# Weight splits three to five slots ahead, background work bounded by the next evictions, and h's buffers moved by 192 bytes

## The chip, the cores and the metric

The kernel runs on one core of one Trainium2 chip. The metric is the device time in microseconds (us) of one execution. The engines are TensorE (PE, matmuls; PEld its weight loads), VectorE (DVE), ScalarE (ACT), GpSimd (POOL) and SyncE (SP, which only issues DMAs here). Each engine works through its own queue in program order and waits at semaphores for the others.

## The reference

For x of 2048 rows and 576 columns, the output is the sum of x, an attention branch and a dense branch, both on the layer-normalised x:

```
xn  = (x - mean(x)) / sqrt(var(x) + 1e-5)
q, k, v = split(xn @ wqkv)                    # 32 heads of 18 columns
o   = softmax(q . k[s - 2j]) v[s - 2j], j=0..7  # 8 keys, two rows apart, masked where s - 2j < 0
out = x + o @ wo + relu(xn @ w1) @ w2         # w1: 576 x 4608, w2: 4608 x 576
```

## The kernel before, in words

**Number format.** Each fp32 operand is written as a high part (rounded for TensorE's fp32r format) and a low part (the rest). A product is high x high + high x low + low x high. Making both parts of a tile is called a split: ScalarE copies the high part, VectorE subtracts it from the source for the low part (function `two`, lines 158 to 164; its VectorE instruction is line 163). Weight tiles are split this way before use: `w1t` (128 x 640, for one block of 128 hidden columns) and `w2t` (128 x 576). The activations h are split on their way out of PSUM: `hhi` by ScalarE with the relu (line 588), `hlo` by VectorE (line 591).

**Slots.** The rows are cut into two phases of 1024 (even and odd rows), each into four blocks of 256 (`tb`). The 4608 hidden columns are cut into 36 tiles of 128; three tiles (`f` = 0, 1, 2) form a chunk. One slot is one hidden tile times one block; a chunk is 12 slots (tb outer, f inner), a phase has 12 chunks, and there are 288 slots, numbered n = 0 to 287. In the body (line 849), slot n issues, in this order:

- the weight splits that are due (`run_splits(n)`);
- half of the h matmuls of a pair of later slots. An even n does the first half for slots n+2 and n+3 together (28 matmuls of 64 rows, two at a time on the two halves of the array), the following odd n the second half (26), and then `hhi` and `hlo` of both;
- in eight slots out of 24, a block of the qkv product (`qkv_tile`, 28 or 26 matmuls of 432 columns, tiles `pm<-wq,xT`);
- `o_two(n)`: 24 matmuls of h(n) with w2 into `po`; at f = 2 VectorE adds the finished `po` to x in four pieces (line 699, `x<-po,x`), which also frees `po` for the next block;
- background work of VectorE (`run_bg`): the attention of one unit of 8 heads, in 77 small steps (products `pr<-qo,k`, sums `lg<-pr`, the softmax on `lg`, products `pr<-lg,v`, tree adds `pr<-pr` and `qo<-pr`). One unit's qkv comes every 24 slots (first at slots 7 to 14 of a phase), and its attention is queued at the 9th slot after.

**What sets the order.** All of it is put out by one Python planner. It keeps two clocks, `t["pe"]` and `t["dve"]`, that grow by a fixed cost for each instruction, and `run_bg(margin)` puts out background steps as long as VectorE's clock would stay within `margin` of TensorE's. The margin is `M` (line 847): 3.0 us after f = 0 and f = 2, 1.5 us after f = 1, and 1.5 us around the product with wo. A split's slot comes from the list `plan` (lines 725 and 726). With s the first slot that uses hidden tile f of a chunk, w1's splits stand at s-5, s-4 and s-2 for f = 0, 1, 2, and w2's at s-3, s-1 and s. In slots counted from the chunk's first slot these are -5, -3, 0 for w1 and -3, 0, 2 for w2. The h matmuls that first use w1's tiles f = 0 and 1 are those of slot -2 of that count, and those that first use f = 2 are those of slot 0. `stage_more` issues a split's DMA into a buffer `st` three splits ahead.

**PSUM.** h has two banks under the name `ph`; a second pair of banks, `pm`, alternates with it except in and right after the slots with a qkv block, where `pm` holds qkv. There each pair of slots uses the same two `ph` banks, so that the next first half waits until `hhi` and `hlo` of the pair before are read out.

Of the kernel before, what the change touches and what calls it, by code (L numbers as in the profile page):

```python
# [10 lines left out]
F32 = mybir.dt.float32  # L11
# [7 lines left out]
P = 128  # L19
# [7 lines left out]
C = 3  # L27
# [5 lines left out]
WO_CHUNK = 10  # L33
# [8 lines left out]
HEADW = (-9, -8, -7, -6, -5, -4)  # L42
# [16 lines left out]
def tile_body(ctx: ExitStack, tc: tile.TileContext, x, wqkv, wo, w1, w2, out):  # L59
# [12 lines left out]
    SPC = NTB * C  # L72
    SPP = NCH * SPC

    ctx.enter_context(tc.manual_schedule())
    pool = lambda name, bufs, **k: ctx.enter_context(tc.tile_pool(name=name, bufs=bufs, **k))
# [7 lines left out]
    w2p = pool("w2p", C + 1)  # L84
    wqp = pool("wqp", 1)
    stp = pool("stp", 5)
    hp = pool("hp", LAG + 1)
    prp = pool("prp", 2)
    lgp = pool("lgp", 1)
# [23 lines left out]
    t = {"pe": 0.0, "dve": 0.0}  # L113
# [16 lines left out]
    def dve(n):  # L130
        t["dve"] += (n + 130) / 960.0
# [16 lines left out]
    def run_splits(n):  # L148
        nonlocal step_now
        while staged and staged[0][0] <= n:  # L150
            step_now, split, st = staged.popleft()
            split(st)
            stage_more()
# [362 lines left out]
    def run_bg(margin):  # L516
        while bg and t["dve"] + bg[0][0] / 960.0 <= t["pe"] + margin:
            n, f, a = bg.popleft()
            f(*a)
            dve(n)  # L520
# [44 lines left out]
    slots = [(ph, c, tb, f) for ph in range(NPH) for c in range(NCH) for tb in range(NTB) for f in range(C)]  # L565
# [34 lines left out]
    def h_mm(n):  # L600
        h_terms(n, TERMS)
        h_out(n)
# [3 lines left out]
    def h_two(g, second):  # L606


        def run(n, terms):
            ph, c, tb, f = slots[n]  # L610
            w, xt = W1[ph, c, f], XT[ph, tb]
            return [
                (HP[n], w[:, b // 5, (b % 5) * P : (b % 5 + 1) * P], xt[:, a, :], not second and j == 0, second and j == len(terms) - 1, TBN)
                for j, (a, b) in enumerate(terms)
            ]

        if not second:
            HB["m"] = not HB["m"] and not busy_m.intersection((g - 3, g - 2, g - 1))
            for n in (g, g + 1):
                HP[n] = ps_m.tile([P, TBN], F32, name="pm") if HB["m"] else ps_h.tile([P, TBN], F32, name="ph")  # L620
            HB["ins"] = mm_rows((run(g, LOWER_MORE), run(g + 1, UPPER_MORE)))
            return
        mm_rows((run(g + 1, LOWER), run(g, UPPER)), HB["ins"])
        h_out(g)
        h_out(g + 1)
# [6 lines left out]
    def o_two(n):  # L632


        ph, c, tb, f = slots[n]
        hi, lo = H.pop(n)
        w = W2[ph, c, f]
        with_wo = c == WO_CHUNK and f == 1
        if f == 0:
            o_tiles(n)  # L640

        def run(k, h, upper):
            cs, first = slice(k * P, (k + 1) * P), k == upper
            z = [(l[:, cs], w[:, b, CUT[h]]) for l, b in ((hi, 0), (hi, 1), (lo, 0))]
            if with_wo:
                more = wo_run(ph, 2 * tb + k, h, (UPPER_MORE if upper else LOWER_MORE) if first else (UPPER if upper else LOWER), upper)
                z = z + more
            return [
                (PO[k, h], l, r, f == 0 and first and j == 0, f == C - 1 and not first and j == len(z) - 1, CUT[h].stop - CUT[h].start)
                for j, (l, r) in enumerate(z)  # L650
            ]

        for j in range(4):
            k, h = divmod(j, 2)
            behind = PB[j - 2] if j > 1 else PB[3] if j == 0 and f else None
            PB[j] = mm_rows((run(k, h, False), run(1 - k, h, True)), behind)
        if with_wo:
            for k in range(2):
                OT.pop((ph, 2 * tb + k))
        o_out(n, rows=True)  # L660
# [25 lines left out]
    def o_out(n, which=range(2), rows=False):  # L686
        ph, c, tb, f = slots[n]
        if f < C - 1:
            return
        end = n == len(slots) - 1  # L690
        order = [(k, h) for k in which for h in range(2)]
        if rows:
            order.sort(key=lambda z: z[1])
        elif end:
            order.sort(key=lambda z: (z[0], -z[1]))
        for k, h in order:
            i = 2 * tb + k
            acc, cols = X[ph, i], CUT[h]
            nc.vector.tensor_tensor(acc[:, cols], PO[k, h], acc[:, cols], op=ALU.add)  # L699
            dve(cols.stop - cols.start)  # L700
            if end and k:
                (nc.scalar if h else nc.sync).dma_start(o_v[ph, i][:, cols], acc[:, cols])
            elif c == NCH - 1 and (k, h) in (order[-1], order[-2 if rows else 1]):
                nc.sync.dma_start(o_v[ph, i], acc)
# [4 lines left out]
    def at(n, f, *a):  # L709
        todo.setdefault(n, []).append((f, a))  # L710
# [3 lines left out]
    def late(n, f, *a):  # L714
        todo_late.setdefault(n, []).append((f, a))

    plan = []
    busy_m = set()
    for ph in range(NPH):
        b = ph * SPP  # L720
        for c in range(NCH):
            for f in range(C):
                s = b + c * SPC + f
                first = ph == c == 0
                plan.append((HEADW[f] if first else s + (-5, -4, -2)[f], w1_task, ((ph, c, f), c * C + f)))
                plan.append((HEADW[3 + f] if first else s + (-3, -1, 0)[f], w2_task, ((ph, c, f), c * C + f)))
        for u in range(NU):
            s = b + UNIT0 + u * UNIT_STEP
            plan.append((s - 5, wq_tasks, ((ph, u), u)))
            for i in range(NI):  # L730
                at(s + i, qkv_tile, ph, u, i)
                busy_m.add(s + i)
            late(s + NI + 1, attention, ph, u)
        plan.append((b + WO_CHUNK * SPC - 6, wo_tasks, (ph,)))
        for i in range(NI):
            z = b + WO_CHUNK * SPC + C * (i // 2) + 1
            out_at, in_at, parts_at = (z + k[i % 2] for k in WO_STEPS)
            late(out_at, wo_a, ph, i)
            late(in_at, wo_f, ph, i)
            at(parts_at, wo_s, ph, i)  # L740
        if ph + 1 < NPH:
            e = b + SPP - SPC
            for i in range(NI):
                if i >= len(XT_STEPS):
                    z = e + 3 + 2 * i - (i == NI - 1)
                    at(z - 6, load_x, ph + 1, i)
                    late(z - 2, stats, ph + 1, i)
                    late(z - 1, norm, ph + 1, i)
                    at(z + 1, make_xt, ph + 1, i)
                    busy_m.add(z + 1)  # L750
                    continue
                load, first, second, send, back, parts = (e + k for k in XT_STEPS[i])
                at(load, load_x, ph + 1, i)
                late(first, stats, ph + 1, i, False, True)
                late(second, norm_turned, ph + 1, i)
                late(send, xt_a, ph + 1, i)
                at(back, xt_f, ph + 1, i)
                at(parts, xt_s, ph + 1, i)
# [70 lines left out]
    h4[0]()  # L829
    h4[1]()  # L830
    o_out(2, (0,))
    x4 = make_xt(0, 4, parts=True)
    for f in x4[:3]:
# [10 lines left out]
        (late if k else at)(z, {"stats": stats, "norm": norm, "xt": make_xt}[op], 0, *a)  # L844
    for tb in range(NTB):
        late((4, 4, 6, 7)[tb], twin, tb)
    M = (3.0, 1.5, 3.0)
    AT_WO = range(WO_CHUNK * SPC - 4, (WO_CHUNK + 1) * SPC)
    for n in range(FIRST, len(slots)):
        run_splits(n)  # L850
        g = n - n % 2 + LAG
        if n < ROW0:
            h_mm(n + LAG)
        elif g < len(slots):
            h_two(g, n % 2 == 1)
        for f, a in todo.pop(n, []):
            f(*a)
        if ROW0 - 1 <= n < len(slots) - C:
            o_two(n)
        else:  # L860
            o_mm(n, n != HALVED)
        if n == HALVED:
            o_out(n, (0,))
        for f, a in todo_late.pop(n, []):
            f(*a)
        if n == HALVED:
            o_out(n, (1,))
        run_bg(1.5 if n % SPP in AT_WO else M[slots[n][3]])
    assert not todo and not todo_late and not bg and not tasks and not staged


# [24 lines left out]
```

## Time and profile before

| | before |
|---|---|
| median of 3 runs | 1310.32 us (1308.1 to 1313.4) |
| the profiled execution | 1312.54 us |
| its span, first to last instruction | 1310.7 us |
| mean granted TensorE clock (1 is 2.4 GHz) | 0.963 |
| busy: PE, PEld, DVE, ACT, POOL | 1203.6, 1182.5, 804.0, 287.1, 44.5 us |

The time of an execution is its span and a small rest around it (1.8 us here). A busy TensorE is not TensorE at its peak: matmuls overlap, and at half the clock the same work is busy for twice as long. The views of the trace that are used further down: the waits of one engine (who waited for whom, in total), the timeline (instructions in order of time, like ones merged; in brackets the idle time before the row and what ended it), and the page.

### The profile page before, as it was taken

The page shows a single profiled execution, that of the slowest core. Times are in us where ns is not written, and L with a number is a line of the kernel's source. Part 1 is how long each engine was busy: PE and PEld are TensorE (multiplying, and loading weights), DVE is VectorE, ACT ScalarE, POOL GpSimd, SP SyncE. Part 2 cuts the span into 40 slices and gives each one's busy share as a digit, 9 for nine tenths or more (in the row PEclk, how much of TensorE's full clock was granted, in tenths as well). Part 3 has the DMA queues.
Part 4 walks back from the last instruction along what each step waited for, and adds up shares of the span by engine and source line. Part 5 has one row for each costly group of instructions (what it writes and reads, how often), then busy time and mean ns, then how long its engine had stood idle before and what let it go on. Part 6 is the DMA issues. An engine that isn't in the chain of part 4 may idle for free.

```text
span 1310.7 us, 38255 instructions
## 1 busy us (share of the span) xinstructions
PE 1203.6 (92%) x17114; PEld 1182.5 (90%) x17114; DVE 804.0 (61%) x1457; ACT 287.1 (22%) x756; POOL 44.5 (3%) x60
## 2 busy tenths in 40 slices
PE   9998989979898998899989989899798989988998
PEld 8998989979898898899979989899798988988998
DVE  7346866775685766753662468576766857667523
ACT  5311212221212111211432121112112121112110
POOL 3100000000000000000010000000000000000000
PEclk9999989999998999999989999898999989999999
DMA  5221212212221211544651222122022212116411
GB/s 173 69 62 42 63 38 66 71 29 61 55 68 31 61 40 49 134 91 110 149 148 40 62 55 68 30 56 79 21 62 55 68 31 61 40 48 141 88 50 74
DMA packets 149939, 89.70 MB, mean 68 GB/s; under 512 B 58528, under 2 KB 133536, under 8 KB 149776
## 3 DMA queue, kind: packets, MB, share of 16 engines
q1 hardware_dynamic: 146816, 78.61, 22.4%
q10 hardware_dynamic: 2960, 8.65, 2.3%
q8 instruction: 134, 2.20, 0.7%
q14 instruction: 29, 0.24, 0.1%
HBM read 67.90 MB, written 11.14 MB: 60 GB/s over the span
## 4 chain that ended last, share of the span: by engine, by line
PE 75%; DVE 17%; issue 2%; DMA 2%; SPq 1%; ACT 1%; POOL 0%; DVEq 0%; POOLq 0%; ACTq 0%
PE po L126 33%; PE pm L126 23%; PE ph L126 18%; DVE x L699 5%; DVE w1t L163 2%; DVE w2t L163 2%; DVE pr L491 2%; DVE lg L464 2%; DVE pr L498 1%; DMA st<-in_w 1%; DVE hlo L591 1%; DVE pr L461 1%; PE po L116 0%; DVE lg L486 0%; SPq L353 0%
## 5 line engine op out<-in xcount | busy, mean ns | idle before, releaser
L126 PE MATMUL po<-w2t,hhi 64*128 64x256 f32 (+1 forms) x4448 | 467.0, 298 | 0.3 <-DVE w2t L163 0.3
L126 PEld LDWEIGHTS po<-w2t,hhi 64*128 64x128 f32 x4448 | 381.6, 190 | 2.4 <-issue 0.8
L126 PE MATMUL ph<-xT,w1t 64*128 64x256 f32 x4698 | 317.8, 280 | 61.6 <-DVE w1t L163 43.0
L126 PEld LDWEIGHTS ph<-xT,w1t 64*128 64x128 f32 x4698 | 301.4, 188 | 68.5 <-DVE w1t L163 46.7
L126 PE MATMUL po<-w2t,hlo 64*128 64x256 f32 (+1 forms) x2224 | 354.0, 297 | 1.2 <-DVE hlo L591 1.2
L699 DVE TENSOR_TENSOR x<-po,x 128x320 f32<-128x320 f32 (+1 forms) x384 | 149.1, 450 | 185.1 <-PE po L126 182.3
L126 PEld LDWEIGHTS po<-w2t,hlo 64*128 64x128 f32 x2224 | 235.6, 190 | 1.6 <-DVE hlo L591 1.6
L126 PE MATMUL pm<-xT,w1t 64*128 64x256 f32 x2808 | 193.2, 285 | 37.2 <-DVE w1t L163 29.1
L126 PEld LDWEIGHTS pm<-xT,w1t 64*128 64x128 f32 x2808 | 181.7, 192 | 43.6 <-DVE w1t L163 31.9
L126 PE MATMUL pm<-wq,xT 64*128 64x432 f32 x1728 | 189.3, 366 | 0.0
L126 PEld LDWEIGHTS pm<-wq,xT 64*128 64x128 f32 x1728 | 170.7, 194 | 3.2
L591 DVE SCALAR_TENSOR_TENSOR hlo<-ph,hhi 128x256 fp32r<-128x256 f32 x183 | 69.3, 419 | 164.5 <-ACT hhi L588 164.4
L588 ACT ACTIVATE hhi<-ph 128x256 fp32r<-128x256 f32 x183 | 60.7, 381 | 344.8 <-PE ph L126 311.4
L588 ACT ACTIVATE hhi<-pm 128x256 fp32r<-128x256 f32 x105 | 34.7, 382 | 299.6 <-PE pm L126 299.5
L591 DVE SCALAR_TENSOR_TENSOR hlo<-pm,hhi 128x256 fp32r<-128x256 f32 x105 | 39.6, 419 | 98.5 <-ACT hhi L588 98.5
L461 DVE TENSOR_TENSOR pr<-qo,k 128x1152 f32<-128x1152 f32 x64 | 85.1, 1351 | 2.5 <-DMA k<-k 2.5
L464 DVE TENSOR_REDUCE lg<-pr 128x64 f32<-128x1152 f32 x64 | 85.4, 1345 | 0.0
L491 DVE TENSOR_TENSOR pr<-lg,v 128x1152 f32<-128x1152 f32 x64 | 84.8, 1353 | 0.3
L430 ACT ACTIVATE k<-pm 128x144 f32<-128x144 f32 x64 | 19.3, 301 | 276.7 <-PE pm L126 276.7
L498 DVE TENSOR_TENSOR pr<-pr 128x288 f32<-128x288 f32 (+1 forms) x128 | 70.7, 603 | 0.0
L163 DVE TENSOR_TENSOR w1t<-st,w1t 128x640 fp32r<-128x640 f32 x70 | 57.3, 818 | 0.4 <-ACT w1t L159 0.3
L159 ACT ACTIVATE w1t<-st 128x640 fp32r<-128x640 f32 x72 | 53.4, 742 | 8.9 <-DMA st<-in_w 8.9
(87 smaller groups left out, 692.0 us busy)
## 6 DMA issues: line engine op xcount, KB each, us to landing
st<-in_w SPq DMA_DIRECT2D x72, 288.0 KB, 3.0
st<-in_w SPq DMA_DIRECT2D x72, 256.0 KB, 3.0
st<-in_wqkv SPq DMA_DIRECT2D x32, 216.0 KB, 3.0
turned<-tr SPq DMA_DIRECT2D x64, 80.0 KB, 2.6
xn<-turned SPq DMA_DIRECT2D x16, 320.0 KB, 3.4
st<-in_w SPq DMA_DIRECT2D x144, 32.0 KB, 2.9
out<-x SPq DMA_DIRECT2D x15, 288.0 KB, 2.5
x<-in_x SPq DMA_DIRECT2D x14, 288.0 KB, 4.5
```

What stands on the lines that cost most here:

```text
L126: ins = nc.tensor.matmul(o, l[z], r[z], start=start, stop=stop)
L159: nc.scalar.activation(hi, src, AF.Copy)
L163: nc.vector.tensor_tensor(lo, src, f32(hi), op=ALU.subtract)
L430: nc.scalar.activation(k[:, W - 1 + j, :], pq[:, 1, :], AF.Copy)
L461: nc.vector.tensor_tensor(pr[i], q, window(k, i), op=ALU.mult)
L464: nc.vector.tensor_reduce(lg[:, i], pr.pop(i).rearrange(heads, d=Dh), axis=AX.X, op=ALU.add)
L491: nc.vector.tensor_tensor(pr[i].rearrange(heads, d=Dh), e, window(v, i).rearrange(heads, d=Dh), op=ALU.mult)
L498: nc.vector.tensor_tensor(o, z[:, 0:n], z[:, n : 2 * n], op=ALU.add)
L588: nc.scalar.activation(hi, pt, AF.Relu)
L591: nc.vector.scalar_tensor_tensor(lo, pt, 0.0, f32(hi), op0=ALU.max, op1=ALU.subtract)
L699: nc.vector.tensor_tensor(acc[:, cols], PO[k, h], acc[:, cols], op=ALU.add)
```

## The change

Four edits, all in the planner's numbers or in a buffer's place; no arithmetic changes.

- Splits: w1's slots become s-5, s-5, s-4 and w2's s-3, s-2, s-2 for f = 0, 1, 2. Counted from the chunk's first slot that is -5, -4, -2 for w1 and -3, -1, 0 for w2: one split in each of six slots.
- Clock: where the planner puts out the adds `x<-po,x` (`o_out`), VectorE's clock is moved up to TensorE's minus 0.4 us, if it is behind that.
- Margins: `margin(n)` takes the place of `M` and of the special case around wo. It is 1.5 or 2.4 us after f = 1 (n even or odd) and 2.2 or 3.2 us after f = 0 and 2, and 2.4 us more where slot n+1 has a qkv block. (The name `odd` in it is true for an even n.)
- Buffers: a pool `gap` of 192 bytes per partition stands between the staging buffers and h's, so that h's buffers and all pools after them (`pr`, `lg` and the small ones) lie 192 bytes further on.

```diff
+    gap = pool("gap", 1)
+    gap.tile([P, 48], F32, name="gap")
     hp = pool("hp", LAG + 1)
...
         end = n == len(slots) - 1
+        t["dve"] = max(t["dve"], t["pe"] - 0.4)
         order = [(k, h) for k in which for h in range(2)]
...
-                plan.append((HEADW[f] if first else s + (-5, -4, -2)[f], w1_task, ((ph, c, f), c * C + f)))
-                plan.append((HEADW[3 + f] if first else s + (-3, -1, 0)[f], w2_task, ((ph, c, f), c * C + f)))
+                plan.append((HEADW[f] if first else s + (-5, -5, -4)[f], w1_task, ((ph, c, f), c * C + f)))
+                plan.append((HEADW[3 + f] if first else s + (-3, -2, -2)[f], w2_task, ((ph, c, f), c * C + f)))
...
-    M = (3.0, 1.5, 3.0)
-    AT_WO = range(WO_CHUNK * SPC - 4, (WO_CHUNK + 1) * SPC)
+    def margin(n):
+
+        odd, qkv = n % 2 == 0, n + 1 in busy_m
+        if slots[n][3] == 1:
+            return (1.5 if odd else 2.4) + 2.4 * qkv
+        return (2.2 if odd else 3.2) + 2.4 * qkv
+
...
-        run_bg(1.5 if n % SPP in AT_WO else M[slots[n][3]])
+        run_bg(margin(n))
```

TensorE's instructions keep their order. On VectorE it changes at three kinds of place, shown for the first unit that has them; the same rows come back every 24 slots. In the changed kernel the lines are two or three further on (L699 is L702, L591 is L593, L163 is L165, L491 is L493).

**Place 1, VectorE, slots 35 and 36**, the first of a chunk, inside the slots with qkv blocks (`x` the adds after slot 35, `pr` and `qo` attention, `w1t` the tile f = 2 that the matmuls of slot 36 need). Before:

```order
L699 TENSOR_TENSOR x<-po,x 128x256 x2
L699 TENSOR_TENSOR x<-po,x 128x320 x2
L491 TENSOR_TENSOR pr<-lg,v 128x1152 x2
L498 TENSOR_TENSOR pr<-pr 128x576
L163 TENSOR_TENSOR w2t<-st,w2t 128x576
L163 TENSOR_TENSOR w1t<-st,w1t 128x640
```

After (from slot 33's last steps on; this `w1t` is the same tile, and the adds are those after slot 35):

```order
L493 TENSOR_TENSOR pr<-lg,v 128x1152 x2
L500 TENSOR_TENSOR pr<-pr 128x576
L165 TENSOR_TENSOR w1t<-st,w1t 128x640
L500 TENSOR_TENSOR pr<-pr 128x576
L500 TENSOR_TENSOR pr<-pr 128x288 x2
L500 TENSOR_TENSOR qo<-pr 128x144 x2
L165 TENSOR_TENSOR w2t<-st,w2t 128x576
L593 SCALAR_TENSOR_TENSOR hlo<-ph,hhi 128x256 x2
L702 TENSOR_TENSOR x<-po,x 128x256 x2
L702 TENSOR_TENSOR x<-po,x 128x320 x2
```

The tile's low part stood behind the adds and three attention steps of slot 35; now it stands in slot 34, ahead of the `hlo` pair of slot 35 and of those adds.

**Place 2, VectorE, slots 44 to 48**, the first of a chunk without qkv blocks (the adds are those after slot 47 before, those after slot 44 and slot 47 after). Before:

```order
L699 TENSOR_TENSOR x<-po,x 128x256 x2
L699 TENSOR_TENSOR x<-po,x 128x320 x2
L461 TENSOR_TENSOR pr<-qo,k 128x1152
L163 TENSOR_TENSOR w2t<-st,w2t 128x576
L163 TENSOR_TENSOR w1t<-st,w1t 128x640
L464 TENSOR_REDUCE lg<-pr 128x64
```

After:

```order
L165 TENSOR_TENSOR w1t<-st,w1t 128x640
L702 TENSOR_TENSOR x<-po,x 128x256 x2
L702 TENSOR_TENSOR x<-po,x 128x320 x2
L165 TENSOR_TENSOR w2t<-st,w2t 128x576
L593 SCALAR_TENSOR_TENSOR hlo<-pm,hhi 128x256 x2
L466 TENSOR_REDUCE lg<-pr 128x64 x2
L165 TENSOR_TENSOR w1t<-st,w1t 128x640
L165 TENSOR_TENSOR w2t<-st,w2t 128x576
L593 SCALAR_TENSOR_TENSOR hlo<-ph,hhi 128x256 x2
L702 TENSOR_TENSOR x<-po,x 128x256 x2
L702 TENSOR_TENSOR x<-po,x 128x320 x2
```

The two `w1t` are the tiles f = 1 (slot 44) and f = 2 (slot 46) of the chunk that begins at slot 48; both now stand ahead of the adds after slot 47.

**Place 3, VectorE, slots 30 and 31**, where a unit's softmax meets the first qkv block (`m`, `lg<-lg,m` and `r` are the softmax; `hlo` is that of slots 32 and 33). Before:

```order
L473 TENSOR_REDUCE m<-lg 128x64
L163 TENSOR_TENSOR w1t<-st,w1t 128x640
L591 SCALAR_TENSOR_TENSOR hlo<-ph,hhi 128x256 x2
L476 TENSOR_TENSOR lg<-lg,m 128x512
L480 TENSOR_REDUCE r<-lg 128x64
```

After:

```order
L475 TENSOR_REDUCE m<-lg 128x64
L478 TENSOR_TENSOR lg<-lg,m 128x512
L482 TENSOR_REDUCE r<-lg 128x64
L165 TENSOR_TENSOR w1t<-st,w1t 128x640
L593 SCALAR_TENSOR_TENSOR hlo<-ph,hhi 128x256 x2
```

Two softmax steps moved ahead of the `hlo` pair, since the margin after slot 30 grew by 2.4 us less 0.8.

## Rows read from the trace of the kernel before

**Rows 1.** The cores view (span, mean clock) and part 1 of the page.

```profile
core 0: 1310.7 us, clock 0.963
...
PE 1203.6 (92%) x17114; PEld 1182.5 (90%) x17114; DVE 804.0 (61%) x1457; ACT 287.1 (22%) x756; POOL 44.5 (3%) x60
```

**Rows 2.** Waits of PE: us in total, times, longest us.

```profile
PE ph L126 <- DVE w1t L163: 43.0, 18, 4.9
PE pm L126 <- DVE w1t L163: 29.1, 14, 2.3
PE ph L126 <- DVE hlo L591: 13.3, 7, 2.1
```

**Rows 3.** Timeline of PE, slots 56 to 73: start, us, instruction, [idle before <-releaser].

```profile
262.49 1.80 PE L126 MATMUL ph<-xT,w1t 64*128 64x256 f32 x28
268.23 1.69 PE L126 MATMUL ph<-xT,w1t 64*128 64x256 f32 x26
276.33 2.08 PE L126 MATMUL ph<-xT,w1t 64*128 64x256 f32 x27 [2.09 <-DVE hlo L591]
282.46 1.69 PE L126 MATMUL ph<-xT,w1t 64*128 64x256 f32 x26
288.29 1.11 PE L126 MATMUL ph<-xT,w1t 64*128 64x256 f32 x16
294.29 1.65 PE L126 MATMUL ph<-xT,w1t 64*128 64x256 f32 x12 [4.88 <-DVE w1t L163]
301.30 0.87 PE L126 MATMUL ph<-xT,w1t 64*128 64x256 f32 x12
...
312.93 1.66 PE L126 MATMUL ph<-xT,w1t 64*128 64x256 f32 x26
316.01 1.77 PE L126 MATMUL pm<-xT,w1t 64*128 64x256 f32 x28
319.21 1.66 PE L126 MATMUL pm<-xT,w1t 64*128 64x256 f32 x26
...
334.87 1.20 PE L126 MATMUL ph<-xT,w1t 64*128 64x256 f32 x17
...
346.65 1.65 PE L126 MATMUL pm<-xT,w1t 64*128 64x256 f32 x12 [2.33 <-DVE w1t L163]
350.56 1.65 PE L126 MATMUL pm<-xT,w1t 64*128 64x256 f32 x26
```

**Rows 4.** Timeline of DVE, slots 54 to 60.

```profile
260.17 0.82 DVE L163 TENSOR_TENSOR w1t<-st,w1t 128x640 fp32r<-128x640 f32 x1
260.90 0.76 DVE L591 SCALAR_TENSOR_TENSOR hlo<-ph,hhi 128x256 fp32r<-128x256 f32 x2
261.56 0.69 DVE L476 TENSOR_TENSOR lg<-lg,m 128x512 f32<-128x512 f32 x1
263.01 1.12 DVE L480 TENSOR_REDUCE r<-lg 128x64 f32<-128x512 f32 x1 [0.76 <-ACT lg L477]
...
275.86 0.75 DVE L591 SCALAR_TENSOR_TENSOR hlo<-ph,hhi 128x256 fp32r<-128x256 f32 x2
...
288.07 1.55 DVE L699 TENSOR_TENSOR x<-po,x 128x256 f32<-128x256 f32 x4 [2.65 <-PE po L126]
289.54 2.62 DVE L491 TENSOR_TENSOR pr<-lg,v 128x1152 f32<-128x1152 f32 x2
...
```

**Rows 5.** Sums by stretch: engines' busy us, then TensorE's granted clock, DMA share, GB/s.

```profile
237.40:292.00 54.60, 49.92 (x720) 49.31 (x718) 38.84 (x65) 12.84 (x36) 2.86 (x3) 1.00 0.19 51
292.00:298.90 6.90, 4.61 (x30) 4.40 (x32) 5.34 (x10) 0.00 (x0) 0.00 (x0) 0.51 0.33 90
```

**Rows 6.** Timeline of PE at the wo product and at the phases' border.

```profile
545.09 1.22 PE L126 MATMUL pm<-xT,w1t 64*128 64x256 f32 x16 [2.31 <-ACT w1t L159]
548.45 1.65 PE L126 MATMUL pm<-xT,w1t 64*128 64x256 f32 x12 [2.14 <-DVE w1t L163]
661.63 3.35 PE L126 MATMUL ph<-xT,w1t 64*128 64x256 f32 x28 [5.39 <-ACT w1t L159]
```

## The prediction

> **What bounds the kernel now.** I read the cores view first, then page part 1, the waits of TensorE, and the timelines of TensorE and VectorE. The profiled execution took 1312.54 us, its span 1310.7 at a mean granted clock of 0.963, with TensorE busy 1203.6 us and VectorE 804.0 [rows 1]. So TensorE sets the time, and what it loses is idle time and time at half clock. VectorE has room on average (38.84 us busy of 54.60 in an ordinary stretch, [rows 5]), yet two of TensorE's three largest waits are for a weight split of VectorE (43.0 us in 18, 29.1 in 14) and the third for `hlo` (13.3 in 7) [rows 2]. Those waits come from order on VectorE, not from its load.
>
> An undisturbed slot is the difference between two starts [rows 3]: odd 312.93 to 316.01 = 3.08 us, even 316.01 to 319.21 = 3.20; with a qkv block, even 262.49 to 268.23 = 5.74, odd 282.46 to 288.29 = 5.83. What a slot takes beyond that is lost. Three places repeat:
>
> - **D**, the chunk's first slot among those with qkv: 288.29 to 301.30 = 13.01, less 5.74 = 7.27 us lost. In it stands a wait of 4.88 for `w1t` [rows 3]; VectorE was at the adds from 288.07 and two `pr<-lg,v` until 292.16 [rows 4], behind which that split stood. The clock then was 0.51 for 6.90 us, its lower level of 1.2 GHz, where the stretch before had 1.00 [rows 5].
> - **C**, two slots before D: 268.23 to 282.46 = 14.23, less 5.83 and 5.74 = 2.66 lost, with a wait of 2.09 for `hlo` [rows 3]. The clock stayed at 1.00 there [rows 5].
> - **B**, a chunk's border without qkv: 334.87 to 350.56 = 15.69, less 3.20, 3.08 and 3.20 = 6.21 lost, with a wait of 2.33 for `w1t` in it [rows 3].
>
> C and D come with the second, third and fourth unit of each phase, six times in all; B at ten chunk borders. Waits of 4.88 six times and 2.33 ten times are 29.3 of the 43.0 and 23.3 of the 29.1 [rows 2], which fits those counts.
>
> **The change part by part.**
>
> *Splits, for D.* The tile f = 2, behind the adds and three attention steps before, now comes two slots ahead of its use. It stands before an `hlo` pair that the same matmuls need anyway, so it can't be last. The whole 7.27 goes, the half clock too, as no wait of that length is left. 6 x 7.27 = 43.6.
>
> *Splits, for B.* Both `w1t` tiles of the next chunk come ahead of the adds at the border, the later one in the second slot before its use, thus about 3 us early by the slots above. 10 x 6.21 = 62.1.
>
> *Splits and clock line, for C.* The adds can start only when TensorE is through with `po`, so a step put out too early in front of `hlo` delays it. With the planner's VectorE clock raised at the adds, between them and `hlo` there are now one `pr<-lg,v` less (2.62 / 2 = 1.31), one `w1t` (0.82) and one step on 128 x 512 (0.69) [rows 4]: 2.8 us against a wait of 2.09. 6 x 2.66 = 16.0, with a margin of only 0.7.
>
> *The wo product.* Twice TensorE waits 2.31 for ScalarE's high part of a `w1t`, whose weight load stands on SP behind other DMAs [rows 6]; a wait of VectorE follows it, about 2 us by what is left of the 29.1 after B (5.8 in four, the two larger taken at 2.1). With half clock as in B (6.21 less 2.33 and a first wait of about 1) I put the place at 2.31 + 2.1 + 2 = 6.4, an estimate. The load is now issued a slot earlier, on SP ahead of those DMAs; I keep 1.5 of it as late. Gain 2 x 4.9 = 9.8.
>
> *The rest.* The 18 waits of 43.0 us, less 29.3 for D, leave 13.7 in twelve; ten belong to B at about 1 each, so two, at the first chunk border of each phase, hold about 3.5. They go by the same move as B. Smaller waits for `w1t` and `hlo` (13.3 less 6 x 2.09 = 0.8, and 1.5 of the 29.1) with their slots: 4, an estimate. At the phases' border TensorE waits 5.39 for ScalarE [rows 6]; its load is issued earlier, but ScalarE takes its work in order, so I count 1.5 and leave the rest.
>
> *Margins: a new wait, E.* Where the softmax of a unit meets its first qkv slots, subtraction and sum (with ScalarE's exponential between them) now stand before `w1t` and the `hlo` pair on which TensorE's next pair waits. From rows of the next unit at that place: subtraction 260.17 for 0.69, wait for ScalarE 0.76, sum from 261.62 for 1.12 [rows 4], split until 263.47, then `hlo`; TensorE went on 0.47 after the start of an `hlo` pair (276.33 after 275.86, [rows 3, 4]), thus at 263.94 instead of 262.49: 1.45 late. It comes six times: 6 x 1.5 = 9.0 lost. The wait of 2.09 in C was followed by full clock [rows 5], so I add no half clock. Bounds: nothing, if the pair has slack that I don't see, and 6 x (1.5 + 3) = 27, with D's half clock (6.90 us that held 3.4 of full-clock work) behind each.
>
> *Buffers 192 bytes on.* Time for `hhi`, `hlo` and the weight loads could change either way. Before shows no other address; but h's rotating buffers lie at different addresses already, and the slots that use them agree: two with qkv from 301.30 to 312.93 took 11.63 [rows 3], against 5.83 + 5.74 = 11.57, 0.03 a slot apart. I take 0, with plus and minus 8 us (0.03 x 280 slots) at the most. The Trainium skill ("SBUF — State Buffer", section Who interferes with whom) says that PE and ACT never wait on anyone in SBUF; by it the edit is worth 0 as well, and no run here shows a shift of 192 bytes.
>
> **Sum.** D 43.6 + B 62.1 + C 16.0 + wo 9.8 + first borders 3.5 + small 4 + border 1.5 = 140.5; less E 9.0 = 131.5. Profiled: 1312.54 - 131.5 = 1181.0. The median of the runs, 1310.32, is 2.2 below the profiled execution, so the forecast is 1179 us, with 1172 to 1188 for this case alone.
>
> The Trainium skill ("Perfetto Trace Analysis", section Identifying the Most-Contended Engine) would judge headroom by the share of weight loads, not of matmuls. That speaks against the size of the sum: with PEld busy 1182.5 of 1310.7 [rows 1], at most 128.2 us could go, which ends at 1182 on the scale of the runs. Here the trace does not hold it as a floor: in the stretch at clock 0.51 the loads were busy 4.40 of 6.90 us at half speed [rows 5], so part of the 1182.5 is itself removed with the half clock. Its result lies within the forecast's own range.
>
> **The rivals.**
>
> - *E is dearer* (chance 0.20). The wait brings half clock, or a `pr` product lands in front of the next `hlo` as well and C comes back under another place. For it: the margins grow by 2.4 just ahead of qkv slots, and C's cover is 0.7 us. Against: the clock stayed full after 2.09. Price 1.5 to 4.5 us more at each of six places (the second wait like C's 2.66, or half clock): 9 to 27 us, thus 1188 to 1206.
> - *E is absent* (0.12): VectorE is far enough ahead at slot 30 that subtraction and sum run while TensorE still works. For it: VectorE's steps before are shorter now that the splits are spread. Then 1179 - 9 = 1170, and with small terms larger 1162 to 1171.
> - *Loads or ScalarE late* (0.06). A split needs its weights; moved up, it can wait for DMA or for ScalarE's copy instead, as at the wo product (2.31) and the phases' border (5.39). If a third of B and D stays: (43.6 + 62.1) / 3 = 35 more, 1214; range 1206 to 1303. Against: each DMA moves up with its split, and the four buffers of a tile are free in time by the order.
> - *Slower, by the shift of h* (0.03). All h buffers, `pr` and `lg` lie on other addresses. If `hlo`, `hhi` or the loads of h into TensorE took longer for it, every slot would pay; it decides against the gain from 131.5 / 280 = 0.47 us in a slot of 3.2 on, and 0.5 gives 1179 + 140 = 1319. Against: the 0.03 us above.
> - *The change doesn't do what it says* (0.03): the splits move, but TensorE then waits for the `hlo` pair at the same places, the matmuls' other input, and the time stays at 1305 to 1315. Against: in D and B `hlo` of the pair was done before the split in the order.
>
> **How the numbers follow.** Forecast 0.56, E dearer 0.20, E absent 0.12, late 0.06, slower 0.03, no effect 0.03. The range 1162 to 1204 holds the first three nearly whole, 0.86, as wide as E's bounds and the shift's 8 us make it. About 0.5% (6.6 us) is what a measurement of this kernel tells from no change; faster than that are the first four, 0.94; within it 0.03; slower 0.03.
>
> **What would show it.** Right: the wait of PE for `w1t` falls from 72 us to under 10, mean clock rises to about 0.99, D's slot takes 5.8, B's three slots 9.5, and `hlo` waits of about 1.5 stand six times in the first qkv slots of a unit. E dearer: stretches at half clock behind those. Shift: an undisturbed even slot other than 3.20. Wrong altogether: waits for `st` or ScalarE in the place of VectorE's, or D and B losing as before.

## The result, and the profile after

The changed kernel takes 1180.58 us (median of 4 runs, 1178.85 to 1182.93) against 1310.01 us for the kernel before (4 runs by now), a ratio of 0.9011 (95% interval 0.8984 to 0.9037). The forecast was 1179. The profiled execution took 1178.85 us, 133.7 less than that of before, where the sum said 131.5.

The cores view and part 1 of the page, to be laid beside [rows 1]:

```profile
core 0: 1177.1 us, clock 1.000
...
PE 1153.4 (98%) x17114; PEld 1140.9 (97%) x17114; DVE 805.3 (68%) x1457; ACT 288.1 (24%) x756; POOL 44.0 (4%) x60
```

The same instructions ran; VectorE's busy time is the same within 1.3 us. The mean granted clock rose from 0.963 to 1.000, and TensorE's busy time fell by 50 us without a matmul fewer. The waits of TensorE, against [rows 2] (us in total, times, longest):

```profile
PE ph L128 <- DVE hlo L593: 10.2, 8, 1.4
PE po L128 <- DVE x L702: 3.2, 4, 1.4
PE po L128 <- ACT k L551: 2.4, 2, 1.7
PE po L109 <- POOL mhalf L104: 1.3, 1, 1.3
PE pm L128 <- ACT w1t L161: 1.3, 2, 1.0
```

No wait for VectorE's `w1t` is left of 72.1 us. Six of the eight waits in the first row are new: they are the wait E that the prediction named. The timeline of TensorE, slots 54 to 61 and then 70 to 73, against [rows 3]:

```profile
230.19 1.76 PE L128 MATMUL ph<-xT,w1t 64*128 64x256 f32 x28
233.36 1.65 PE L128 MATMUL ph<-xT,w1t 64*128 64x256 f32 x26
240.69 2.21 PE L128 MATMUL ph<-xT,w1t 64*128 64x256 f32 x28 [1.39 <-DVE hlo L593]
246.80 1.69 PE L128 MATMUL ph<-xT,w1t 64*128 64x256 f32 x26
252.66 1.82 PE L128 MATMUL ph<-xT,w1t 64*128 64x256 f32 x28
258.44 1.69 PE L128 MATMUL ph<-xT,w1t 64*128 64x256 f32 x26
264.29 1.77 PE L128 MATMUL ph<-xT,w1t 64*128 64x256 f32 x28
270.00 1.67 PE L128 MATMUL ph<-xT,w1t 64*128 64x256 f32 x26
...
303.29 1.76 PE L128 MATMUL ph<-xT,w1t 64*128 64x256 f32 x28
306.46 1.65 PE L128 MATMUL ph<-xT,w1t 64*128 64x256 f32 x26
309.52 1.76 PE L128 MATMUL pm<-xT,w1t 64*128 64x256 f32 x28
312.70 1.65 PE L128 MATMUL pm<-xT,w1t 64*128 64x256 f32 x26
```

Slot 60, the place D, takes 264.29 to 270.00 = 5.71 where it took 13.01. The place B, 303.29 to 312.70, takes 9.41 where it took 15.69. C (slots 57 and 58) takes 246.80 to 258.44 = 11.64 where it took 14.23. E stands where the forecast put it: slots 55 and 56 take 233.36 to 246.80 = 13.44, against 5.83 + 5.74 = 11.57 undisturbed. VectorE in front of it, against [rows 4]:

```profile
235.80 1.15 DVE L475 TENSOR_REDUCE m<-lg 128x64 f32<-128x512 f32 x1 [1.26 <-POOL lg L469]
236.98 0.69 DVE L478 TENSOR_TENSOR lg<-lg,m 128x512 f32<-128x512 f32 x1
238.43 1.14 DVE L482 TENSOR_REDUCE r<-lg 128x64 f32<-128x512 f32 x1 [0.76 <-ACT lg L479]
239.48 0.82 DVE L165 TENSOR_TENSOR w1t<-st,w1t 128x640 fp32r<-128x640 f32 x1
240.21 0.76 DVE L593 SCALAR_TENSOR_TENSOR hlo<-ph,hhi 128x256 fp32r<-128x256 f32 x2
```

Subtraction and sum, with the wait of 0.76 between them, now come ahead of `w1t` and `hlo`, and TensorE goes on 0.48 us after `hlo` starts. The sums by stretch of the slots 54 to 62, against [rows 5]:

```profile
230.20:281.90 51.70, 50.31 (x687) 49.82 (x686) 39.42 (x68) 11.55 (x39) 2.85 (x3) 1.00 0.17 48
```

The clock is 1.00 right through a stretch that holds both E and D.

### The profile page after: what moved, and what is told of

It is laid out like the page before. It is cut to its first block, busy times and chain, and to the rows that moved or that the text cites. A ratio compares the mean times of both kernels' runs of the same rounds, so it can differ in the third digit from the quotient of the medians.

```text
span 1177.1 us, 38332 instructions
## 1 busy us (share of the span) xinstructions
PE 1153.4 (98%) x17114; PEld 1140.9 (97%) x17114; DVE 805.3 (68%) x1457; ACT 288.1 (24%) x756; POOL 44.0 (4%) x60
## 4 chain that ended last, share of the span: by engine, by line
PE 91%; DVE 3%; DMA 2%; SPq 1%; issue 1%; ACT 1%; POOL 0%; DVEq 0%; POOLq 0%; ACTq 0%
PE po L128 40%; PE pm L128 27%; PE ph L128 22%; DMA st<-in_w 1%; DMA xn<-turned 1%; PE po L118 1%; DVE x L702 1%; DVE w1t L165 1%; SPq L355 0%; PE po L109 0%; PE pm L302 0%; PE ph L118 0%; DVE hlo L593 0%; SPq L177 0%; DVE xT L310 0%
## 5 line engine op out<-in xcount | busy, mean ns | idle before, releaser
L128 PE MATMUL po<-w2t,hhi 64*128 64x256 f32 (+1 forms) x4448 | 452.6, 292 | 3.2 <-DVE x L702 3.2
L128 PEld LDWEIGHTS po<-w2t,hhi 64*128 64x128 f32 x4448 | 365.6, 184 | 6.8 <-issue 3.4
L128 PE MATMUL po<-w2t,hlo 64*128 64x256 f32 (+1 forms) x2224 | 341.4, 290 | 0.0
L128 PE MATMUL ph<-xT,w1t 64*128 64x256 f32 x4698 | 302.8, 275 | 10.3 <-DVE hlo L593 10.2
L128 PEld LDWEIGHTS ph<-xT,w1t 64*128 64x128 f32 x4698 | 290.3, 184 | 13.6 <-DVE hlo L593 12.3
L702 DVE TENSOR_TENSOR x<-po,x 128x320 f32<-128x320 f32 (+1 forms) x384 | 149.0, 450 | 153.1 <-PE po L128 150.2
L128 PEld LDWEIGHTS po<-w2t,hlo 64*128 64x128 f32 x2224 | 225.0, 185 | 0.0
L128 PE MATMUL pm<-wq,xT 64*128 64x432 f32 x1728 | 180.5, 354 | 0.0
L128 PE MATMUL pm<-xT,w1t 64*128 64x256 f32 x2808 | 178.3, 274 | 1.3 <-ACT w1t L161 1.3
L128 PEld LDWEIGHTS pm<-xT,w1t 64*128 64x128 f32 x2808 | 172.0, 184 | 1.8 <-ACT w1t L161 1.8
L593 DVE SCALAR_TENSOR_TENSOR hlo<-ph,hhi 128x256 fp32r<-128x256 f32 x183 | 69.3, 419 | 92.7 <-ACT hhi L590 92.7
L493 DVE TENSOR_TENSOR pr<-lg,v 128x1152 f32<-128x1152 f32 x64 | 85.1, 1350 | 0.2
L593 DVE SCALAR_TENSOR_TENSOR hlo<-pm,hhi 128x256 fp32r<-128x256 f32 x105 | 39.7, 419 | 50.3 <-ACT hhi L590 48.9
L165 DVE TENSOR_TENSOR w1t<-st,w1t 128x640 fp32r<-128x640 f32 x70 | 57.2, 817 | 13.3 <-ACT w1t L161 12.8
L165 DVE TENSOR_TENSOR w2t<-st,w2t 128x576 fp32r<-128x576 f32 x72 | 54.0, 750 | 17.4 <-ACT w2t L161 17.4
```

What stands on the lines that cost most here:

```text
L128: ins = nc.tensor.matmul(o, l[z], r[z], start=start, stop=stop)
L165: nc.vector.tensor_tensor(lo, src, f32(hi), op=ALU.subtract)
L493: nc.vector.tensor_tensor(pr[i].rearrange(heads, d=Dh), e, window(v, i).rearrange(heads, d=Dh), op=ALU.mult)
L593: nc.vector.scalar_tensor_tensor(lo, pt, 0.0, f32(hi), op0=ALU.max, op1=ALU.subtract)
```

## The experiments

Place by place, the table gives what the slots took beyond the undisturbed lengths of before (3.20, 3.08, 5.74, 5.83 us), summed over the whole execution from each kernel's trace. A negative number means slots shorter than those. Each of the eight slots with the product with wo holds about 7.1 us more of matmuls in every one of these kernels; that work is left out.

| place | before | after | splits alone | all but the splits | without E |
|---|---|---|---|---|---|
| D | 43.9 | -0.3 | 0.3 | 44.5 | -0.2 |
| B | 62.4 | -0.9 | 0.2 | 46.8 | -1.0 |
| C | 17.5 | 0.3 | 9.6 | 1.3 | -0.2 |
| E | 0.0 | 11.5 | 2.5 | 3.2 | -0.4 |
| wo product | 12.8 | 9.5 | 9.6 | 11.3 | 9.5 |
| phases' border | 9.2 | 2.7 | 4.1 | 6.7 | 2.6 |
| first borders of the phases | 4.0 | -0.2 | 0.0 | 3.8 | -0.2 |
| all slots | 162.0 | 27.8 | 32.8 | 127.4 | 15.4 |

**Splits alone.** Only the slots of the splits, on the kernel before:

```diff
-... s + (-5, -4, -2)[f], w1_task ...      s + (-3, -1, 0)[f], w2_task ...
+... s + (-5, -5, -4)[f], w1_task ...      s + (-3, -2, -2)[f], w2_task ...
```

> Only the splits' slots are those of the change; clock, margins and buffers as before. If the splits' places carry the gain: D, B and the first borders are gone (110 us); between the adds and hlo at C about 1.1 us of steps fewer than before, so C keeps a wait of about 1.0 six times instead of 2.09, and E's wait is about 0.5 instead of 1.4, since one lg sum is put out a slot earlier: 1173 to 1190 us, about 1179. Rival, C hangs on the clock line: its 17.5 us stay, 1195 to 1202.

1183.29 us, ratio to before 0.904 (0.9012 to 0.9068). So 126 of the 129 us come with the splits. The one wait at C, in the timeline of TensorE, slots 57 to 59:

```profile
246.38 1.69 PE L126 MATMUL ph<-xT,w1t 64*128 64x256 f32 x26
253.39 2.21 PE L126 MATMUL ph<-xT,w1t 64*128 64x256 f32 x28 [0.99 <-DVE hlo L591]
259.53 1.69 PE L126 MATMUL ph<-xT,w1t 64*128 64x256 f32 x26
```

It is 0.99 us where 1.0 was expected. C does not hang on the clock line as a whole: the splits alone take nearly half of it away, and 9.6 of 17.5 us stay without the other edits.

**All but the splits.** The change with the two tuples of before.

> The change with the splits back in their old slots (clock line, margins and gap stay). If the splits carry D and B: D's 44 us stay, of B's 62 about 50 (the two lg sums in front of its first wait are gone, the pr product in front of its second is not), C's 17.5 go and E's 11.5 do not come: 1275 to 1295 us, waits of 4.9 for w1t six times. Rival, the bound on background work alone keeps VectorE free for the splits in time: under 1230.

1280.11 us, ratio 0.9779 (0.9748 to 0.981). D is as before, in TensorE's timeline of slots 60 and 61, and so is B's larger wait, at slot 72:

```profile
281.34 1.10 PE L128 MATMUL ph<-xT,w1t 64*128 64x256 f32 x16
287.55 1.65 PE L128 MATMUL ph<-xT,w1t 64*128 64x256 f32 x12 [5.10 <-DVE w1t L165]
294.29 1.67 PE L128 MATMUL ph<-xT,w1t 64*128 64x256 f32 x26
...
337.87 0.97 PE L128 MATMUL pm<-xT,w1t 64*128 64x256 f32 x12 [2.32 <-DVE w1t L165]
```

Bounding the background work does not bring a split forward: D lost 44.5 us, B 46.8 of 62.4. The clock line and margins together do take C away (1.3 left). So D, the first borders and most of B are the splits' affair; C goes by clock line and margins together wholly, by the splits by nearly half. The gains do not add up: these other edits alone bring 29 us, the splits alone 126, and all of them 129, since both take away C and part of B.

**Without the gap.** The change without the pool of 192 bytes.

> The change without the 192 bytes of gap. If the shift is worth nothing: 1178 to 1184 us, plain slots 3.17 and 3.06 as with the gap, or 3.20 and 3.08 as before. Rival, the shift is behind the 0.02 to 0.03 us by which plain slots are now shorter: 280 slots x 0.025 = 7 us more, 1185 to 1190.

1185.48 us, ratio 0.9061 (0.9035 to 0.9087): the rival. Even and odd plain slots (those without qkv) are 3.20 and 3.09 us, as before; with the gap they are 3.17 and 3.06. The two intervals of the ratio just overlap (the change's ends at 0.9037), so it is the slots that decide here. This was followed up below.

**Without E.** The 2.4 us of margin only where slot n has a qkv block as well:

```diff
-        odd, qkv = n % 2 == 0, n + 1 in busy_m
+        odd, qkv = n % 2 == 0, n in busy_m and n + 1 in busy_m
```

> The change, with the 2.4 us of margin given only where slot n has a qkv block too, so that maximum, subtraction and sum of the softmax come behind the hlo pair in front of a unit's first qkv slot. If E is what is left of the steps put out too early: waits for hlo fall from 10.2 us to under 4, slots 31, 55, 79 and their twins lose nothing, 1167 to 1172 us. Rival, the steps pushed back delay the next hlo pair or w1t instead: waits of 1 to 2 us in slots 57 or 60, 1177 to 1185.

1169.30 us, ratio 0.8935 (0.8907 to 0.8963). TensorE's slots 55 to 57, and VectorE ahead of slot 56:

```profile
231.19 1.65 PE L128 MATMUL ph<-xT,w1t 64*128 64x256 f32 x26
236.96 1.79 PE L128 MATMUL ph<-xT,w1t 64*128 64x256 f32 x28
242.67 1.67 PE L128 MATMUL ph<-xT,w1t 64*128 64x256 f32 x26
```

```profile
232.30 0.81 DVE L165 TENSOR_TENSOR w1t<-st,w1t 128x640 fp32r<-128x640 f32 x1
233.32 0.76 DVE L593 SCALAR_TENSOR_TENSOR hlo<-ph,hhi 128x256 fp32r<-128x256 f32 x2 [0.21 <-ACT hhi L590]
234.10 1.15 DVE L475 TENSOR_REDUCE m<-lg 128x64 f32<-128x512 f32 x1
```

The same three softmax steps stand behind `hlo`, and the two slots take 11.48 us instead of 13.44. The steps pushed back delayed nothing: six times 1.96 is 11.8, and the median fell by 11.3.

**Where h lies.** Five kernels, with the expectations below in this order: gap behind h, 384 bytes, the gap alone on the kernel before, 64 bytes, 256 bytes. The gap behind h's buffers, in the kernel without E:

```diff
-    gap = pool("gap", 1)
-    gap.tile([P, 48], F32, name="gap")
     hp = pool("hp", LAG + 1)
+    gap = pool("gap", 1)
+    gap.tile([P, 48], F32, name="gap")
```

The other three sizes (64, 256 and 384 bytes are 16, 64 and 96 columns):

```diff
-    gap.tile([P, 48], F32, name="gap")
+    gap.tile([P, 96], F32, name="gap")
```

And the gap alone, on the kernel before:

```diff
     stp = pool("stp", 5)
+    gap = pool("gap", 1)
+    gap.tile([P, 48], F32, name="gap")
     hp = pool("hp", LAG + 1)
```

> The kernel without wait E (1169.3 us), with the 192 bytes behind h's buffers instead of ahead of them: h lies where it lay before, pr, lg and the small buffers lie as in the change. If h's own place is what shortens plain slots (3.17 and 3.06 with it, 3.20 and 3.09 without): 3.20 and 3.09 come back, 1173 to 1177 us. Rival, the place of pr, lg and what follows does it (VectorE's traffic): 3.17 and 3.06, 1167 to 1171.

> The kernel without wait E, with a gap of 384 bytes instead of 192. If any shift away from the old place does: plain slots 3.17 and 3.06, 1167 to 1171 us. Rival, 192 is special (or the effect comes by the address modulo some power of two): 3.20 and 3.09, 1173 to 1177, or lower still.

> The kernel before with the 192 bytes alone. If the place of h shortens every slot by 0.02 to 0.03 us whatever the order of the splits: plain slots 3.17 and 3.06, 280 x 0.025 = 7 us at most, 1302 to 1306 us with waits for w1t as before (72 us). Rival, the waits swallow it (a shorter slot only lengthens the wait behind it): 1307 to 1311.

> The kernel without wait E, with a gap of 64 bytes. Seen so far: shift 0 gives plain even slots of 3.20, 192 of 3.17, 384 of 3.25. If only the place that 384 gives is bad: 3.17 to 3.20, 1169 to 1174 us. Rival, the slot goes down evenly from 0 to 192: 3.19, 1171 to 1173; nothing excludes a worse place (3.25, 1183 to 1187).

> The kernel without wait E, with a gap of 256 bytes. If the cost rises evenly from 192 to 384: 3.17 + 0.08 / 3 = 3.20, 1173 to 1177 us. Rival, 384 alone is bad: 3.17, 1168 to 1171.

The row of 192 bytes is the kernel without E. The slots are medians of those without a wait. The rows were not all timed beside the same runs of the kernel before (medians 1309.41, 1306.77 and 1310.33), so the ratio compares them better than the microseconds.

| h's buffers further on by | even, odd plain slot, us (medians) | median of the runs, us | ratio to before (95%) |
|---|---|---|---|
| 0 (gap behind h) | 3.20, 3.09 | 1173.68 | 0.8978 (0.8962 to 0.8994) |
| 64 | 3.16, 3.12 | 1173.20 | 0.8957 (0.8938 to 0.8976) |
| 192 | 3.17, 3.06 | 1169.30 | 0.8935 (0.8907 to 0.8963) |
| 256 | 3.20, 3.09 | 1173.63 | 0.8961 (0.8943 to 0.8978) |
| 384 | 3.25, 3.13 | 1185.39 | 0.907 (0.9052 to 0.9088) |
| 192, alone on the kernel before | 3.17, 3.06 | 1305.26 | 0.997 (0.9953 to 0.9986) |

Three consecutive slots of TensorE, even, odd, even, first of the changed kernel, then of the one without its gap, then of the one with 384 bytes:

```profile
199.02 1.76 PE L128 MATMUL pm<-xT,w1t 64*128 64x256 f32 x28
202.19 1.65 PE L128 MATMUL pm<-xT,w1t 64*128 64x256 f32 x26
205.25 1.76 PE L128 MATMUL ph<-xT,w1t 64*128 64x256 f32 x28
```

```profile
199.75 1.80 PE L126 MATMUL pm<-xT,w1t 64*128 64x256 f32 x28
202.94 1.69 PE L126 MATMUL pm<-xT,w1t 64*128 64x256 f32 x26
206.03 1.80 PE L126 MATMUL ph<-xT,w1t 64*128 64x256 f32 x28
```

```profile
199.77 1.81 PE L128 MATMUL pm<-xT,w1t 64*128 64x256 f32 x28
203.03 1.69 PE L128 MATMUL pm<-xT,w1t 64*128 64x256 f32 x26
206.15 1.81 PE L128 MATMUL ph<-xT,w1t 64*128 64x256 f32 x28
```

No row has a wait, yet the slots differ: 6.23, 6.28 and 6.38 us for the two. With the gap behind h, where only the later pools move, the slots are those without a gap; so it is the place of h. 256 bytes came out as an even rise from 192 to 384 would have it; 384 itself is dearer than either of its expectations. With 64 bytes the time lies in the range expected, but not by slots of the expected lengths: an even slot gains and an odd one loses. The time does not follow the distance, and why the place matters stays open. The 5 us that the gap takes off the kernel before show in the same lengths, 3.17 and 3.06, with the waits for `w1t` unchanged (72.8 us).

**Without the clock line.** The change without `t["dve"] = max(t["dve"], t["pe"] - 0.4)`.

> The change without the line that moves VectorE's planner clock up at the adds. By the order the steps between the adds and hlo at C are 2.9 us instead of 4.0, so C stays gone, and E stays (an lg sum earlier, reciprocal and product more in front of hlo): 1178 to 1186 us. Rival, the line is what removes C: 9.6 to 17.5 us come back, 1190 to 1198.

1176.89 us, ratio 0.9007 (0.899 to 0.9023), just below the expected range and not told apart from the change by the times. C stays away in the trace (0.4 us lost), E stays (10.4). So with the new margins and splits the line is not what removes C; the line without the new margins was not tried.

**Weights staged earlier.** The kernel without E, and `AHEAD = 4` instead of 3.

> The kernel without wait E, with weight loads staged four splits ahead instead of three, which puts the load of w1t f = 2 at the wo product ahead of the DMAs turned<-tr on SP. If that load is what keeps 9.5 us at the two wo products: ScalarE gets it about 3 us earlier, 2 to 3 us less twice, 1163 to 1167 us. Rival, the adds and hlo there are late by VectorE's own work, or the fifth buffer is not free in time: 1168 to 1175.

1169.43 us, ratio 0.8946 (0.8931 to 0.8961): no gain. The `w1t` load does go out earlier, and at the first wo product the waits for `w1t` and for the adds are gone. TensorE then waits for `k`, the product's left operand. TensorE's timeline, and ScalarE's:

```profile
487.29 0.58 PE L128 MATMUL po<-wq,k 64*128 64x256 f32 x1 [3.08 <-ACT k L551]
```

```profile
486.50 0.74 ACT L551 ACTIVATE k<-xn 128x640 fp32r<-128x640 f32 x1 [7.49 <-DMA xn<-turned]
```

So two chains meet at this place, the weights and the attention output, which is transposed through DMAs; with the first out of the way the second ends last. It also came later than without the earlier load: the first copy to `k` starts 8.1 us after the start of slot 120, where it starts after 6.8 in the kernel without E, and in the trace the two places lose about 4 us more than the 9.5 of that kernel. That the earlier load itself pushes those DMAs back was not shown.

**Without E and without the clock line.**

> The change without wait E and without the clock line. If the line is not needed with the new margins: E stays away (maximum and subtraction, but not the sum, stand ahead of hlo, an lg sum earlier), C stays away, and the 2.9 us that the change lost in slots 105 and 249, which the kernel without the clock line did not lose, are saved: 1165 to 1168 us. Rival, without the line steps come too early in front of another hlo: 1169 to 1175.

1164.07 us (1163.13 to 1166.25), ratio to before 0.8888 (0.8869 to 0.8906), just below the expected range. This is the fastest kernel of the study, 16.5 us below the changed one, whose interval begins at 0.8984. The two waits of the change in slots 105 and 249 (2.9 us in all) are gone too (-0.1). The other 2 us or so below the kernel without E are not explained: the profiled executions of the two took 1166.25 and 1166.99 us, and in them the second wo product cost about 2 us more without the line.

## Why the prediction was right

The mechanism was right: the waits went with the order on VectorE, at the same work. Not every term was. By its own steps, the forecast first and then the gain of each place in the traces (before less after, from the table):

- **D**, 43.6 forecast: 44.2. The wait of 4.88 and the half clock behind it both went, and the kernel with all but the splits shows them back at 5.10.
- **B**, 62.1: 63.3. The split two slots ahead was in time at all ten borders.
- **C**, 16.0: 17.2. The steps counted between the adds and `hlo` did decide it: 1.1 us fewer (the splits alone) left 0.99 of 2.09, and 2.7 us fewer (the change) left none.
- **E**, -9.0: -11.5. The mechanism and the place were right, the wait 1.39 against 1.45; the term was sized by the wait alone, while a pair of slots lost 1.96 us (slot 56 itself, behind the wait, took 6.11 us against 5.71 without it). Full clock behind it was right.
- **First borders**, 3.5: 4.2.
- **The wo product**, 9.8: 3.3. This step failed. The size of the place was right (6.4 us each, 12.8 in the table), but the step took the weight load's earlier place on SP as nearly enough, with 1.5 us left of each; 9.5 / 2 = 4.75 stayed. The load does not stand ahead of all the DMAs there: four `turned<-tr` still come before it. ScalarE waited 6.03 us for it, and VectorE, in order, stood behind it with the adds, on which TensorE now waits. SP, ScalarE, VectorE and TensorE there:

```profile
476.97 2.02 SPq L355 DMA_DIRECT2D turned<-tr  x4
479.09 0.47 SPq L173 DMA_DIRECT2D st<-in_w  x1
```

```profile
483.78 0.74 ACT L161 ACTIVATE w1t<-st 128x640 fp32r<-128x640 f32 x1 [6.03 <-DMA st<-in_w]
```

```profile
484.55 0.83 DVE L165 TENSOR_TENSOR w1t<-st,w1t 128x640 fp32r<-128x640 f32 x1 [4.18 <-ACT w1t L161]
...
487.33 1.54 DVE L702 TENSOR_TENSOR x<-po,x 128x256 f32<-128x256 f32 x4
```

```profile
487.89 0.74 PE L128 MATMUL po<-w2t,hhi 64*128 64x256 f32 x4 [1.41 <-DVE x L702]
```

- **The phases' border**, 1.5: 6.5. Under-sized: ScalarE's order did not hold the tile up. It was copied at 589.37, while TensorE came to slot 144 at about 593.3 and then waited 0.98 us for `hlo`, where it had waited 5.39 [rows 6]:

```profile
589.37 0.74 ACT L161 ACTIVATE w1t<-st 128x640 fp32r<-128x640 f32 x1 [3.28 <-DMA st<-in_w]
```

```profile
594.26 2.34 PE L128 MATMUL ph<-xT,w1t 64*128 64x256 f32 x28 [0.98 <-DVE hlo L593]
```

- **Buffers**, 0 within 8 us: worth about 5 us. Without the gap the change takes 4.9 us more, and alone it takes 5 off the kernel before (interval 1.8 to 6.2 us). The sign that the prediction named came: an undisturbed even slot of 3.17 where it was 3.20. The argument that h's rotating buffers already lie at different addresses did not carry over: each is 256 columns of 4 bytes, so they lie 1 KB apart, and a shift of 192 bytes is no such step. By the Trainium skill ("SBUF — State Buffer", section Who interferes with whom) this edit was worth nothing; whatever the cause, the slots here differ, and the measurement decides.

The rest, 4 forecast, came to 7 of the 134.2 of all slots. The gap's 5 us have no place of their own in this list: the slots are a little shorter in all of them, which is part of D's, B's and C's surplus and most of that of the rest. So four terms were off: wo by -6.5, E by -2.5, the border by +5.0, the buffers by +5. That they nearly cancel is luck, and the total of 133.7 against 131.5 hides it. The weight-load rule of "Perfetto Trace Analysis" in the Trainium skill would have allowed 128.2 us, by the prediction's estimate; 133.7 went, and the loads' busy time itself fell by 41.6 us (1182.5 to 1140.9) with the same 17114 loads, as the prediction argued from the half clock.

Of the rivals, a dearer E was right in its sign: 2.5 us more, where it was priced at 9 at least. "Slower by the shift of h" fell for 192 bytes, but not as a mechanism: with 384 bytes the kernel without E takes 12 us more than with h in its old place (1185.39 against 1173.68), and 16 more than with 192.

What the other edits brought: the splits alone take 1183.29 us, and the gap is worth 5, so clock line and margins together come out at about nothing, or a small loss (the change without its gap takes 1185.48). They take 9.3 us of C away and give 9.0 to E.

## What to carry to other kernels

When one engine feeds another through a queue in program order, ask of each input where it stands in that queue and what stands ahead, not how busy the engine is: four slot numbers in a list bring 126 us by themselves, of 129 for the whole change, at an unchanged 805 us of VectorE work. A wait that is removed by pushing optional work away comes back wherever that work is let in again: bound it before each hand-over, the first of a series too. A long wait costs more than its length where the clock falls behind it (7.27 us in D for a wait of 4.88, with the clock at 0.51), so price it by the slot and not by the wait.

## What the hardware did that was not expected

The place of a matmul operand in SBUF changed TensorE's rate without any wait in the trace: 3.17, 3.20 and 3.25 us for the same slot with h moved by 192, 0 and 384 bytes, and 3.16 beside 3.12 for even and odd with 64. At 384 bytes the 28 h matmuls of an even slot were further apart (1.54 us from the start of the first to that of the last, against 1.49 with 192 bytes, means of over 90 slots each), although those matmuls read x and w1, which had not moved. What causes it was not found.
